# Loading two small matrices on 128 partitions, and a load split in two parts, in the opening of an attention and FFN kernel

## The chip, the cores and the metric

The kernel runs on one core of one Trainium2 chip. The metric is the time of one execution on the device in microseconds (us), lower is better; each kernel is run several times. The profile's own span is about 1.8 us shorter than that time (482.0 us for an execution of 483.81 us). In the lines below PE is the TensorE matmul engine, PEld its weight load, DVE the VectorE, ACT the ScalarE, POOL the GpSimd engine, SP the SyncE; L123 is a line of the kernel, and the line numbers shift by a few from one kernel to the next.

## The reference

```python
# batch = 8, heads = 8, seq = 1024, head_dim = 64, k_proj = 64, d_ff = 2048
k_proj = einsum('ks,bhsd->bhkd', E, k)          # E, F: 64 x 1024, float32
v_proj = einsum('ks,bhsd->bhkd', F, v)
attn   = softmax(q @ k_proj^T / 8)              # over the 64 projected keys
x      = (attn @ v_proj) as (8192 tokens, 512)
out    = relu(x @ w_in)**2 @ w_out              # 512 -> 2048 -> 512
```

## The kernel before

It works batch by batch. While the FFN of one batch runs on PE, the attention of the next one is slipped in between its products. Only the first batch has nothing to hide behind: its attention must be computed before the first FFN product. This stretch, about the first 37 us, is called the opening here. In the opening, K, V and Q of batch 0 arrive in pieces, and small "filler" products keep PE at work between them.

```python
e_f32 = []
for src in (E, F):                                    # 64 partitions, 4 KB in each
    t = relu_pool.tile([KP, S], F32, tag="h_relu", name="e_f32")
    nc.sync.dma_start(t[:], src[:])
    e_f32.append(t)
...
def load_heads(t, src, g):                            # four of the eight heads, f32 to bf16 on the way
    s = slice(4 * g, 4 * g + 4)
    nc.gpsimd.dma_start(t[:, s], rows(src, 0)[:, s])

for g in range(2):
    load_heads(K_first, k, g)
...                                                   # half of Q
for g in range(2):
    load_heads(V_first, v, g)
...                                                   # then w_in in 8 pieces, more of Q, w_out

def E_and_F():                                        # bf16, then turned so that s is on partitions
    for t, src, copy in ((ET, e_f32[0], nc.vector.tensor_copy), (FT, e_f32[1], nc.scalar.copy)):
        e_bf = soft_pool.tile([KP, S], BF16, tag="expT", name="e_bf")
        copy(e_bf[:], src[:])
        ps = ffn_psum("ps_E", (P, NI, KP), BF16)
        view = e_bf[:].rearrange("k (p i) -> k i p", i=NI)
        for i in range(NI):
            nc.tensor.transpose(ps[:, i, :], view[:, i, :], ident[0:KP, 0:KP])
        copy(t[:], ps[:])

def first_stages(self):                               # cut
    filler(2)                                         # 128 x 512 products on ET, result unused
    self.project_k(0)                                 # ps_k: 8 products on K's first half
    filler(1)
    self.transpose_k(0)
    self.project_k(1)                                 # K's second half
    filler(2)
    self.transpose_k(1)
    filler(1)
    ...                                               # Q transposes, scores, exponentials
    self.project_v(0); self.copy_v(0)                 # ps_v: 16 products on V's first half
    self.half_sums(0, apart=True); self.half_sums(1)
    self.half_reciprocals(0); self.half_reciprocals(1)
    self.half_values(0)
    self.half_normalize(0, 0, 0)                      # writes xT, which the FFN reads
    self.project_v(1); self.copy_v(1)                 # V's second half
    self.half_normalize(0, 0, 1)

def last_of_first(self):                              # called after the first three FFN products
    self.half_values(1)
    self.half_normalize(0, 1, 0); self.half_normalize(0, 1, 1)

PIECES = {                                            # batches 3 to 7: which FFN step a piece precedes
    ... 23: "sums 0, values 0 0, reciprocals 0", 26: "normalize 0 0",
    28: "scores 2, scores 3, exponentials 2", ...
}
```

The softmax here doesn't subtract the row's maximum and nothing guards it: scores larger than these inputs give would overflow.

## Time and profile before

| | before |
|---|---|
| time, median of 3 runs | 484.76 us (484.01 to 484.77) |
| PE busy | 470.4 us, 98% of the span |
| first product on K's first half | 8.61 us |
| first FFN product | 20.01 us |
| start of the 16th FFN product | 23.70 us |

The page's summary of the kernel before, first the busy time of the engines, then the chain of work that ended last:

```profile
PE 470.4 (98%) x3614; PEld 293.1 (61%) x3614; DVE 313.2 (65%) x380; ACT 261.8 (54%) x414; POOL 33.2 (7%) x46
...
PE 93%; DVE 3%; ACT 2%; DMA 1%; issue 0%; SPq 0%
```

PE is the limit, and nearly all of the waiting that is left lies in the opening. The timeline of the kernel before over its first 24 us follows. A line gives the start, the busy time (both us), engine, line, operation, what is written from what, the shape, how often, and in brackets how long the engine had been idle and what ended it.

```profile
0.74 0.58 SPq L87 DMA_DIRECT2D e_f<-in_E_dram  x1
1.25 1.64 POOL L94 DMA_DIRECT2D K_sb<-in_k_dram  x2 [0.80 <-POOLq L735]
...
4.63 0.89 DVE L137 CAST e_bf<-e_f 64x1024 bf16<-64x1024 f32 x1 [3.73 <-DMA e_f<-in_E_dram]
...
5.91 1.04 ACT L137 CAST e_bf<-e_f 64x1024 bf16<-64x1024 f32 x1 [3.89 <-DMA e_f<-in_F_dram]
...
7.64 1.03 PE L360 MATMUL ps_fill<-ET 128*128 128x512 bf16 x2
...
8.61 1.92 PE L260 MATMUL ps_k<-K_sb,ET 128*64 128x256 bf16 x8
...
11.61 1.42 PE L260 MATMUL ps_k<-K_sb,ET 128*64 128x256 bf16 x8
...
14.23 1.06 PE L295 MATMUL ps_q<-ident,Q_sb 128*128 128x128 bf16 x16
...
18.07 0.30 PE L319 MATMUL ps_att<-expT,ones 64*32 64x256 bf16 x8 [0.21 <-ACT expT L313]
...
18.58 1.06 PE L282 MATMUL ps_v<-V_sb,FT 128*64 128x256 bf16 x16
...
20.01 0.81 PE L459 MATMUL ps_h<-xT,w_in 128*128 128x512 bf16 x3 [0.37 <-DVE xT L350]
```

E and F land at about 4.6 and 5.9 us, are cast by DVE and ACT, and then turned on PE. Two fillers follow. The line for the first `ps_k` products has no bracket: PE did not wait for K, whose first half had landed at 8.25 us. Note also that eight `ps_k` products take 1.92 us in the first group and 1.42 us in the second: the clock of PE doubled within the second group (products start 213 ns apart, then, from about 12.4 us on, 109 ns). The clock row of the page does not show this; it stands at its highest digit in all 40 slices. The Trainium skill, "TensorE: Matmul & The Clock Gate", Part 1, describes this warm-up and says it needs a busy window of about 3.4 us whose phase differs from run to run; the trace agrees with the doubling.

The chain of waits of the kernel before, in order of time (start, length, what), says the same: up to 8.6 us it runs through F's load and the work on it, not through K.

```profile
1.38 4.51 DMA e_f<-in_F_dram
...
5.91 1.05 ACT e_bf L137
...
7.71 0.96 PE ps_fill L360 x2
8.68 1.86 PE ps_k L260 x8
```

### The profile page before, as it was taken

To read this page: it belongs to the slowest core of one execution; us is meant where nothing else is said; L and a number is where in the kernel's file an instruction comes from. 1 tells how busy PE (TensorE), PEld (TensorE's weight loads), DVE (VectorE), ACT (ScalarE), POOL (GpSimd) and SP (SyncE) were. 2 spreads that over 40 slices of the span, in tenths; PEclk is the share of its full clock that TensorE was granted. 3 is DMA by queue.
4 is the path that set the end of the run, shared out by engine and by line. 5 is a ranking of instruction groups with operands and counts; after the bars stand their busy time and mean duration, and the time that the engine had idled before them with its cause. 6 is when DMAs were issued, how large, how long until landed. Compare 5 with 4: busy or idle time off the path is not lost.

```text
span 482.0 us, 8383 instructions
## 1 busy us (share of the span) xinstructions
PE 470.4 (98%) x3614; PEld 293.1 (61%) x3614; DVE 313.2 (65%) x380; ACT 261.8 (54%) x414; POOL 33.2 (7%) x46
## 2 busy tenths in 40 slices
PE   4899999999999999999999999999999999999997
PEld 2544776475575746657475665747557474666656
DVE  1478855555958558493876748666594855948383
ACT  2488544758426664466635657176662756545351
POOL 6340020020020001000010000100000000000000
PEclk9999999999999999999999999999999999999999
DMA  9999989479989075931859147590712002020202
GB/s 162 204 204 207 170 184 203 124 128 227 172 124 238 6 176 89 192 80 64 145 87 229 13 121 131 90 196 1 173 3 81 20 1 88 1 88 0 88 0 88
DMA packets 72501, 55.46 MB, mean 115 GB/s; under 512 B 33936, under 2 KB 64656, under 8 KB 72464
## 3 DMA queue, kind: packets, MB, share of 16 engines
q0 software_dynamic: 30336, 29.36, 39.0%
q1 hardware_dynamic: 42128, 25.56, 21.2%
q8 instruction: 28, 0.46, 0.4%
q14 instruction: 9, 0.07, 0.0%
HBM read 59.24 MB, written 16.78 MB: 158 GB/s over the span
## 4 chain that ended last, share of the span: by engine, by line
PE 93%; DVE 3%; ACT 2%; DMA 1%; issue 0%; SPq 0%
PE ps_h L459 44%; PE ps_y L479 23%; PE ps_z L479 11%; PE ps_x L479 6%; PE ps_kv L178 3%; PE ps_att L219 2%; PE ps_att L204 2%; DVE hsq L518 1%; DMA e_f<-in_F_dram 1%; PE ps_k L260 1%; DVE s L473 1%; DVE xT L244 0%; ACT expT L313 0%; DVE xT L350 0%; ACT h_relu L510 0%; PE ps_fill L360 0%
## 5 line engine op out<-in xcount | busy, mean ns | idle before, releaser
L459 PE MATMUL ps_h<-xT,w_in 128*128 128x512 bf16 x1024 | 225.0, 379 | 0.4 <-DVE xT L350 0.4
L518 DVE TENSOR_TENSOR hsq<-h_relu 128x1024 bf16<-128x1024 f32 x123 | 150.0, 1223 | 76.7 <-ACT h_relu L510 76.1
L510 ACT ACTIVATE h_relu<-ps_h 128x512 f32<-128x512 f32 x256 | 149.8, 597 | 62.6 <-PE ps_h L459 62.4
L459 PEld LDWEIGHTS <-w_in 128*128 128x128 bf16 x1024 | 99.6, 98 | 117.9 <-issue 1.7
L479 PEld LDWEIGHTS <-s 128*128 128x128 bf16 x1024 | 98.5, 98 | 19.8 <-issue 8.7
L479 PEld LDWEIGHTS <-hsq 128*128 128x128 bf16 x768 | 73.8, 98 | 16.4 <-issue 2.9
L479 PE MATMUL ps_y<-T,s 128*128 128x256 bf16 x512 | 62.4, 273 | 0.0
L595 DVE TENSOR_TENSOR o_sb<-ps_z,p_b 128x512 f32<-128x512 f32 x16 | 11.1, 691 | 54.7 <-ACT p_b L591 21.1
L473 DVE TENSOR_TENSOR s<-hsq 128x1024 bf16<-128x1024 bf16 x64 | 43.5, 684 | 0.0
L591 ACT COPY o_sb<-ps_y 128x512 f32<-128x512 f32 x15 | 8.8, 586 | 54.2 <-PE ps_y L479 54.1
L211 ACT ACTIVATE expT<-ps_att 128x1024 bf16<-128x1024 f32 x28 | 27.2, 1025 | 14.0 <-PE ps_att L204 14.0
L244 DVE TENSOR_TENSOR xT<-ps_att,rs 128x1024 bf16<-128x1024 f32 x28 | 33.4, 1216 | 0.6 <-PE ps_att L219 0.6
L479 PE MATMUL ps_x<-w_out,hsq 128*128 128x256 bf16 x256 | 33.2, 273 | 0.0
L479 PE MATMUL ps_y<-w_out,hsq 128*128 128x256 bf16 x256 | 33.2, 273 | 0.0
L479 PE MATMUL ps_y<-T,hsq 128*128 128x256 bf16 x256 | 30.9, 272 | 0.0
L479 PE MATMUL ps_z<-T,s 128*128 128x256 bf16 x256 | 30.6, 273 | 0.0
L479 PE MATMUL ps_z<-w_out,s 128*128 128x256 bf16 x256 | 30.6, 273 | 0.0
L591 ACT COPY p_b<-ps_y 128x512 f32<-128x512 f32 (+1 forms) x17 | 9.4, 556 | 25.9 <-PE ps_y L479 25.8
L473 DVE TENSOR_TENSOR s<-s,hsq 128x1024 bf16<-128x1024 bf16 x32 | 21.9, 686 | 0.3
L473 DVE TENSOR_TENSOR s<-hsq,s 128x1024 bf16<-128x1024 bf16 x32 | 21.8, 684 | 0.0
L81 POOL DMA_DIRECT2D Q_sb<-in_q_dram x7 | 6.1, 877 | 226.1 <-DMA qT<-Q_sb 225.7
L591 ACT COPY p_a<-ps_y 128x512 f32<-128x512 f32 (+1 forms) x17 | 9.4, 561 | 21.8 <-PE ps_y L479 21.6
(74 smaller groups left out, 232.0 us busy)
## 6 DMA issues: line engine op xcount, KB each, us to landing
out_dram<-o_sb SPq DMA_DIRECT2D x30, 512.0 KB, 3.1
K_sb<-in_k_dram POOLq DMA_DIRECT2D x7, 1024.0 KB, 15.4
V_sb<-in_v_dram POOLq DMA_DIRECT2D x7, 1024.0 KB, 22.4
Q_sb<-in_q_dram POOLq DMA_DIRECT2D x7, 1024.0 KB, 9.8
w_in<-in_moe_w_in_dram POOLq DMA_DIRECT2D x8, 256.0 KB, 13.6
w_out<-in_moe_w_out_dram POOLq DMA_DIRECT2D x4, 512.0 KB, 13.3
K_sb<-in_k_dram POOLq DMA_DIRECT2D x2, 512.0 KB, 7.9
V_sb<-in_v_dram POOLq DMA_DIRECT2D x2, 512.0 KB, 12.7
```

The source lines that it names most:

```text
L178: nc.tensor.matmul(ps[0:KP, :], lhsT=ET[:, i, :], rhs=kv[:, :, i, :], start=f, stop=l)
L204: nc.tensor.matmul(ps[o, bank, :], lhsT=self.kT[r, 2 * pr + j, :], start=True, stop=True, rhs=self.qT[r, NT * (2 * pr + j):NT * (2 * pr + ...
L211: nc.scalar.activation(e[:], self.ps["s", pr][:], AF.Exp, scale=SCALE)
L219: nc.tensor.matmul(ps[32 * j:32 * j + 32, a, :], lhsT=weights(o, 4 * g + j), rhs=self.exp[2 * g + j // 2][o, bank, :], start=True, stop=Tr ...
L244: nc.vector.tensor_tensor(out=self.xT[:, 2 * g + e].rearrange("p a n t -> p a (n t)"), in0=self.ps["v", g, e][:], in1=self.rs[g][:], op=AL ...
L459: nc.tensor.matmul(ps[:], lhsT=w_in_blk(cb, fb), rhs=xT[:, cb, :, 2 * ch:2 * ch + 2], start=(cb == 0), stop=(cb == NCB - 1),)
L473: nc.vector.tensor_tensor(out=s[o][:, js], in0=x, in1=y, op=op)
L479: nc.tensor.matmul(ps[tb] if len(ps) == 2 else ps[0][:, tb], lhsT=lhs[:, j, tb * P:(tb + 1) * P], rhs=rhs[:, j], start=first and n == 0 an ...
L510: nc.scalar.activation(r[:, n], ps[:], AF.Relu)
L518: multiply = lambda: nc.vector.tensor_tensor(out=o, in0=r[:], in1=r[:], op=ALU.mult)
L591: nc.scalar.copy(to[:, t], ps)
L595: nc.vector.tensor_tensor(out=to[:, t], in0=ps, in1=more[:, t], op=ALU.add)
```

## The change

The intent: get E and F, which head that chain, in and turned sooner, by loading each on all 128 partitions (2 KB in each instead of 4 KB in 64), where the casts have half as many columns; put in two more fillers, so that PE is at work until K lands; let V's second half and the first piece of w_in arrive in two parts each, so that work can begin on the first part; and bring all four normalizing steps of the opening in front of the FFN, so that its first 16 products run in a row. Two small ones: one ReLU goes from ACT to DVE, and in the later batches "normalize 0 0" is called one FFN step earlier.

```diff
     for src in (E, F):
-        t = relu_pool.tile([KP, S], F32, tag="h_relu", name="e_f32")
-        nc.sync.dma_start(t[:], src[:])
+        t = relu_pool.tile([P, S // 2], F32, tag="h_relu", name="e_f32")
+        nc.sync.dma_start(t[:], src.rearrange("k (c s) -> (k c) s", c=2))
...
-    for g in range(2):
-        load_heads(V_first, v, g)
+    for s in (slice(0, 4), slice(4, 6), slice(6, 8)):
+        load_heads(V_first, v, s)
...
-            nc.gpsimd.dma_start(w_in_sb[j][:, g], w_in_view[:, g, :, j * fw:(j + 1) * fw])
+            for n in range(2) if (j, g) == (0, 0) else (slice(None),):
+                s = slice(n * fw // 2, (n + 1) * fw // 2) if n in (0, 1) else n
+                nc.gpsimd.dma_start(
+                    w_in_sb[j][:, g, :, s], w_in_view[:, g, :, j * fw:(j + 1) * fw][:, :, s])
...
+        pick = ident[:].rearrange("p (k c) -> p c k", c=2)
...
-            e_bf = soft_pool.tile([KP, S], BF16, tag="expT", name="e_bf")
+            e_bf = soft_pool.tile([P, S // 2], BF16, tag="expT", name="e_bf")
             copy(e_bf[:], src[:])
-            ps = ffn_psum("ps_E", (P, NI, KP), BF16)
-            view = e_bf[:].rearrange("k (p i) -> k i p", i=NI)
+            ps = ffn_psum("ps_E", (P, NI, KP))
+            view = e_bf[:].rearrange("r (p i) -> r i p", i=NI)
             for i in range(NI):
-                nc.tensor.transpose(ps[:, i, :], view[:, i, :], ident[0:KP, 0:KP])
+                for c, o in enumerate((LO, HI)):
+                    nc.tensor.matmul(ps[o, i, :], lhsT=view[:, i, :], rhs=pick[:, c, :], start=True, stop=True)
...
-            filler(2)
+            filler(4)
...
-            self.half_normalize(0, 0, 0)
-            self.project_v(1)
-            self.copy_v(1)
-            self.half_normalize(0, 0, 1)
-
-        def last_of_first(self):
+            for s in heads[1:]:                       # slice(4, 6), slice(6, 8)
+                self.project_v(s)
+                self.copy_v(s)
             self.half_values(1)
-            self.half_normalize(0, 1, 0)
-            self.half_normalize(0, 1, 1)
+            for g in range(2):
+                for e in range(2):
+                    self.half_normalize(0, g, e)
...
-        23: "sums 0, values 0 0, reciprocals 0", 26: "normalize 0 0",
+        23: "sums 0, values 0 0, reciprocals 0", 25: "normalize 0 0",
...
-                nc.scalar.activation(r[:, n], ps[:], AF.Relu)
+                if (b, ch, k, n) == (0, 0, 0, 1):
+                    nc.vector.tensor_scalar_max(r[:, n], ps[:], 0.0)
+                else:
+                    nc.scalar.activation(r[:, n], ps[:], AF.Relu)
```

## The prediction

> **What bounds it now.** TensorE. The page gives PE 98% busy; the chain of waits is 93% PE. From 37 us on, the timeline shows products back to back (0.216 us per 512 columns). Only the first 37 us and small holes later can give anything; 2% (9.7 us) is out of reach.
>
> The opening is paced by loads. DMA issues and landings, in order: K 8.25 and 10.86, Q 13.50, V 16.00 and 18.54, w_in 19.88, 21.97, 23.00, 24.29 us: 2.5 us per 512 KB, DMA share full from 4.5 us. The Trainium skill ("DMA: Bandwidth & Descriptors", Issuing engines are not separate DMA queues) says that all DMAs share the same 16 engines, so splitting a load brings no bandwidth, only an earlier first part; the trace agrees (Q's shorter rows moved at K's rate).
>
> **What the change does.**
> 1. E, F on 128 partitions: casts 0.89 (DVE) and 1.04 us (ACT) should fall to about 0.5 and 0.6; but 16 products each instead of 8 transposes, and the ET copy reads f32 (0.43 -> about 0.65). FT is ready 0.3 to 0.5 us earlier, ET about as before. Two more fillers (0.43 us each, cold) last until K lands. Steadier work may warm the TensorE clock earlier. The Trainium skill ("TensorE: Matmul & The Clock Gate", Part 1) has the clock double after a free-running busy window of about 3.4 us. The trace agrees in kind: K products start 213 ns apart until 12.2 us, 109 after. Warm at the first K group would save 0.85 us there, so the Q transposes start near Q's landing (13.55 instead of 14.23), and the first reciprocals end up to 0.7 us earlier than 19.24.
> 2. V split: but the last V part still lands at 18.5. Then products (0.45 + 0.2), copy (0.3), and DVE now does both V copies before the first normalize, which so starts at about 19.5 (before: 19.27). The first FFN product starts at about 20.2, LATER than 20.01. In exchange the second values (0.34 us at 20.75) come before it, so the 16 opening products end about 0.2 us earlier (last start 23.70 -> 23.47). The wait for the first ReLU stays; the next stage starts at about 23.9 instead of 24.11. w_in landings (24.29, 28.18) leave only 0.25 us of slack, so no more can be passed on unless the loads themselves come earlier.
> 3. w_in's first piece in halves: lands before it is needed; about 0. ReLU on DVE (about 0.7 us): first square about 0.3 us earlier, off the path.
> 4. "normalize 0 0" one step earlier in the later batches. There the second scores group waits for DVE's xT to free PSUM: the scores take 0.636 instead of 0.559 us (timeline at 166.0 us). Before the o_sb add, DVE ends it in time. 0.08 us x 5 batches = 0.39 us.
>
> **Sum.** 0.2 (opening) + 0.39 (later batches) = 0.6: 484.76 - 0.6 = 484.1 us, range 483.3 to 484.8. Chances: faster 0.01, same 0.98, slower 0.01.
>
> **Right if:** first ps_h product at about 20.2 with 16 in a row; the 37 us point about 0.2 to 0.3 us earlier; those later scores no longer wait for xT; last V landing unmoved.
>
> **Wrong if:** 2 KB rows make E and F slow and push K and all later landings back; or they speed them and all shifts up; the clock warms no earlier and fillers delay K's products; run-to-run spread (0.76 us) hides it all.

## The result, and the profile after

The changed kernel took 485.29 us (median of 5 runs, 484.52 to 485.43), the kernel before 484.76 us in the same comparison (5 runs, 484.01 to 485.00). The ratio is 1.0012, with a 95% interval of 0.9998 to 1.0025. A ratio here is always the mean time of one kernel's fast runs over that of the other's of the same rounds, so it is not quite the ratio of the medians quoted beside it. The change did not gain 0.6 us: it lost a few tenths, and the median lies outside the predicted range. The interval of this comparison just includes no change at all; that of the repetition `after_again` (below) does not.

The same stretch of the timeline, kernel after:

```profile
0.75 0.39 SPq L87 DMA_DIRECT2D e_f<-in_E_dram  x1
...
1.25 1.63 POOL L93 DMA_DIRECT2D K_sb<-in_k_dram  x2 [0.80 <-POOLq L738]
...
3.47 0.70 DVE L142 CAST e_bf<-e_f 128x512 bf16<-128x512 f32 x1 [2.56 <-DMA e_f<-in_E_dram]
...
4.18 0.62 ACT L142 CAST e_bf<-e_f 128x512 bf16<-128x512 f32 x1 [2.16 <-DMA e_f<-in_F_dram]
...
6.42 1.89 PE L364 MATMUL ps_fill<-ET 128*128 128x512 bf16 x4
...
8.92 1.87 PE L265 MATMUL ps_k<-K_sb,ET 128*64 128x256 bf16 x8 [0.61 <-DMA K_sb<-in_k_dram]
...
11.87 1.71 PE L265 MATMUL ps_k<-K_sb,ET 128*64 128x256 bf16 x8
...
14.79 1.06 PE L299 MATMUL ps_q<-ident,Q_sb 128*128 128x128 bf16 x16
...
19.08 1.08 PE L287 MATMUL ps_v<-V_sb,FT 128*64 128x128 bf16 x32
...
21.15 5.11 PE L462 MATMUL ps_h<-xT,w_in 128*128 128x512 bf16 x22 [0.19 <-DVE xT L354]
```

The first half of it is what was wanted, and more. E and F land 1.2 and 1.7 us earlier, and even with twice as many fillers PE is done with them at 8.3 us. But K's first half, issued at the same 1.25 us as before, now lands at 8.88 us, 0.63 us later than before. PE stands idle for 0.61 us and starts on K 0.31 us later than in the kernel before. The second group of K's products then takes 1.71 us instead of 1.42, because the clock doubles about 0.9 us later (by the spacing of the products between 13.15 and 13.31 us, instead of between 12.25 and 12.42). Together that is 0.56 us at the Q transposes, and it is still there when V's products begin. The chain of waits, kernel after, now starts with K's load, and after it nothing but work follows:

```profile
1.25 7.62 DMA K_sb<-in_k_dram
...
8.92 1.88 PE ps_k L265 x8
...
11.94 1.65 PE ps_k L265 x8
...
16.64 1.95 ACT expT L317 x2
...
18.63 0.52 PE ps_att L323 x24
19.15 1.03 PE ps_v L287 x32
...
20.21 0.29 DVE vp L291
20.50 0.61 DVE xT L354
...
21.15 3.61 PE ps_h L462 x16
...
30.41 23.23 DMA V_sb<-in_v_dram
```

The last line is a second place: V of batch 1 lands at 53.64 us (before 52.48), and this time PE waits for it. The two timelines at that place, before and then after:

```profile
52.44 0.40 PE L178 MATMUL ps_kv<-K_sb,ET 128*64 128x512 bf16 x1
52.53 0.38 PE L179 MATMUL ps_kv<-V_sb,FT 128*64 128x512 bf16 x1
```

```profile
53.12 0.40 PE L183 MATMUL ps_kv<-K_sb,ET 128*64 128x512 bf16 x1
53.69 0.38 PE L184 MATMUL ps_kv<-V_sb,FT 128*64 128x512 bf16 x1 [0.16 <-DMA V_sb<-in_v_dram]
```

A product on K and one on V start 0.09 us apart before and 0.57 us apart after, so this wait costs 0.48 us. One DMA engine alone makes it: fifteen of the sixteen (see "The experiments") had delivered their share of V by 52.76 us, before PE asked for it at about 53.2, and the last came 0.89 us after them. This lag is not yet there in the last load before K of batch 1 (w_out, all sixteen by 42.64 us); in between a 16 KB packet of the instruction queue began at 42.67 us and took 0.89 us. So this loss most likely belongs to that packet and not to the loads of E and F; the trace does not say which engine the packet ran on, so it is not shown. And a third place, the one that was meant to gain, does gain. In the five later batches, the scores of heads 4 to 7 no longer wait for DVE to free their PSUM (timeline of PE in batch 2, before and then after; the next product starts 0.64 us after the scores began, then 0.56 us):

```profile
165.99 0.70 PE L204 MATMUL ps_att<-qT,kT 64*64 64x512 bf16 x8
166.63 1.05 PE L479 MATMUL ps_x<-w_out,hsq 128*128 128x256 bf16 x8
```

```profile
167.14 0.63 PE L209 MATMUL ps_att<-qT,kT 64*64 64x512 bf16 x8
167.70 1.05 PE L482 MATMUL ps_x<-w_out,hsq 128*128 128x256 bf16 x8
```

How far the kernel after lags behind, when the same product of the two traces is compared: 0.69 us at 37 us, 1.15 us from 55 to 140 us, 0.76 us at 425 us, 0.72 us in the span. So the opening cost 0.69, the wait for V another 0.48, and the later scores gave 0.39 back.

### The profile page after: what moved, and what is told of

It reads as the page before. It is cut to its first block, busy times and chain, and to the rows that moved or that the text cites. A ratio compares the mean times of both kernels' runs of the same rounds, so it can differ in the third digit from the quotient of the medians.

```text
span 482.7 us, 8459 instructions
## 1 busy us (share of the span) xinstructions
PE 472.4 (98%) x3648; PEld 294.5 (61%) x3648; DVE 314.4 (65%) x382; ACT 260.9 (54%) x413; POOL 34.5 (7%) x48
## 4 chain that ended last, share of the span: by engine, by line
PE 89%; DMA 6%; DVE 3%; ACT 1%; issue 0%; POOLq 0%
PE ps_h L462 41%; PE ps_y L482 23%; PE ps_z L482 11%; PE ps_x L482 6%; DMA V_sb<-in_v_dram 5%; PE ps_kv L183 2%; PE ps_att L224 2%; PE ps_att L209 2%; DMA K_sb<-in_k_dram 2%; DVE hsq L524 1%; PE ps_k L265 1%; DVE s L476 1%; DVE xT L249 0%; ACT expT L317 0%; PE ps_kv L184 0%
## 6 DMA issues: line engine op xcount, KB each, us to landing
w_out<-in_moe_w_out_dram POOLq DMA_DIRECT2D x4, 512.0 KB, 13.2
```

## The experiments

Every load here runs on 16 DMA engines, each of which reports when its share is done; a load has landed when the sixteenth has. The Trainium skill, "DMA: Bandwidth & Descriptors", section "Why a DMA increments its semaphore by 16 and not by 1", says that these engines finish independently, and the traces show it. The sixteen completions of K's first half, sorted, read from the completion records of the traces (us):

```
before   7.51 7.53 7.58 7.65 7.65 7.70 7.71 7.73 7.77 7.78 7.91 7.92 7.95 8.04 8.22 8.25   spread 0.74
after    6.92 6.98 7.00 7.01 7.01 7.05 7.06 7.12 8.66 8.67 8.75 8.83 8.85 8.86 8.87 8.88   spread 1.96
```

After the change eight engines are done with K earlier than any was before, and eight later than any was before. K's bytes did not get slower as a whole (the mean of the sixteen is 7.81 and 7.91 us; in the four later profiles with such loads and K issued at 1.25 us it is 7.14, 7.58, 7.73 and 8.56); the engines fell out of step, and the slowest decides. Nor do they get wholly back in step: the loads queue up behind one another, and the spread of the later ones is still 1.2 to 1.3 us (V's last part 18.19 to 19.42 us; in the kernel before V's last half has 0.52). "Spread" below means the time from the first to the last of the sixteen completions of K's first half.

The theory to be tested: E and F on 128 partitions, in flight while K's load starts, put the 16 engines out of step; this delays K and everything behind it. Its rivals: the split loads and the new order of the opening cost the time (then E and F are innocent); or the spread has another cause, which the tables of each experiment name. Where an expectation calls a theory by a letter, the sentence ahead of it or the text itself says which is meant. Several expectations count on V's last landing plus some 1.7 us for the first FFN product; the section on the prediction says where that holds.

Three (`no_load`, `ef_tiny`, `ef_gap`) are single runs, and only their traces are used. Medians in us, the kernel before being run again in each batch on the same chip:

| kernel | K's 1st half lands | spread | V's last part lands | 1st / 16th FFN product | median | before, same batch | ratio (95%) |
|---|---|---|---|---|---|---|---|
| before | 8.25 | 0.74 | 18.54 | 20.01 / 23.70 | | | |
| after | 8.88 | 1.96 | 19.42 | 21.15 / 24.38 | 485.29 | 484.76 | 1.0012 (0.9998 to 1.0025) |
| ef_only | 9.53 | 2.69 | 19.87 | 21.70 / 25.39 | 485.82 | 484.06 | 1.0032 (1.0017 to 1.0048) |
| no_ef | 8.52 | 1.20 | 18.83 | 20.50 / 23.88 | 485.00 | 484.06 | 1.0014 (0.9998 to 1.0029) |
| norm_only | 8.21 | 0.82 | 18.50 | 20.34 / 24.02 | 484.27 | 484.06 | 1.0000 (0.9987 to 1.0014) |
| after_again | 9.73 | 2.98 | 20.08 | 21.78 / 25.02 | 485.19 | 484.06 | 1.0024 (1.0009 to 1.0040) |
| pool_wait | 9.64 | 2.98 | 20.15 | 21.76 / 25.44 | 486.07 | 484.86 | 1.0027 (1.0014 to 1.0039) |
| quiet | 9.88 | 3.12 | 20.15 | 24.85 / 28.54 | 488.81 | 484.86 | 1.0083 (1.0070 to 1.0096) |
| no_load | 6.90 | 0.60 | 17.37 | 18.98 / 22.67 | 482.76 | 484.86 | one run |
| norm_wait | 8.77 | 1.58 | 19.07 | 20.45 / 24.14 | 484.22 | 484.86 | 0.9994 (0.9980 to 1.0008) |
| halves | 8.45 | 1.25 | 18.73 | 20.12 / 23.82 | 484.34 | 484.25 | 0.9997 (0.9981 to 1.0012) |
| ef_late | 6.92 | 0.62 | 18.84 | 24.89 / 28.58 | 488.51 | 484.25 | 1.0078 (1.0063 to 1.0094) |
| ef_pool | 10.69 | 3.07 | 21.46 | 23.12 / 26.36 | 485.84 | 484.25 | 1.0031 (1.0013 to 1.0048) |
| f_late | 8.27 | 1.68 | 19.36 | 21.89 / 25.12 | 483.93 | 484.25 | 0.9993 (0.9977 to 1.0010) |
| rows2k | 7.94 | 0.78 | 18.24 | 20.47 / 24.15 | 484.26 | 484.33 | 0.9998 (0.9980 to 1.0017) |
| ef_tiny | 7.29 | 0.63 | 17.57 | 20.05 / 23.75 | 483.80 | 484.33 | one run |
| ef_gap | 10.52 | 0.51 | 21.31 | 23.64 / 27.34 | 487.34 | 484.33 | one run |
| halves_rest | 9.27 | 1.98 | 19.59 | 21.75 / 25.00 | 483.72 | 484.33 | 0.9986 (0.9973 to 1.0000) |
| halves_rest2 | 8.24 | 1.01 | 18.60 | 20.27 / 23.68 | 483.74 | 484.16 | 0.9994 (0.9982 to 1.0007) |
| rows2k_rest | 8.04 | 1.37 | 18.35 | 20.44 / 23.67 | 484.73 | 484.16 | 1.0009 (0.9995 to 1.0023) |

The columns on K, V and FFN products come from one profiled run each, the medians from 1 to 6 runs. A profiled run can lie at the edge of its kernel's runs: those of `halves_rest` (484.91 us), `pool_wait` and `ef_late` are their slowest, those of `after`, `no_ef`, `norm_only`, `halves`, `rows2k`, `halves_rest2` and `rows2k_rest` their fastest. The kernel before itself ranged from 483.64 to 485.60 us over the 51 runs of these five batches, with a median of 484.30.

### First question: which part of the change costs the time?

`ef_only` is the kernel before with the E and F part of the change alone, and the four fillers:

```diff
-        t = relu_pool.tile([KP, S], F32, tag="h_relu", name="e_f32")
-        nc.sync.dma_start(t[:], src[:])
+        t = relu_pool.tile([P, S // 2], F32, tag="h_relu", name="e_f32")
+        nc.sync.dma_start(t[:], src.rearrange("k (c s) -> (k c) s", c=2))
   (and the casts, the products on pick and filler(4), as in the change)
```

> The kernel before with only the E and F part of the change (128 partitions, 16 products each, four fillers). Theory D (the early end of the E and F loads makes K start into a rough stretch: K lands later although E and F land earlier): K's halves land at about 8.9 and 11.7 us, last V at about 19.4, and the time is 0.3 to 0.8 us over before. Theory S (the splitting of V and w_in is what slows the loads): K lands at 8.25 or earlier, last V at 18.5 or earlier, time equal to before or 0.1 to 0.3 us less. Theory C (chance: one DMA engine falls behind at random or by the fetch of instructions): landings unlike both, no pattern over the kernels.

It lost 1.5 us on average (ratio 1.0032), no less than the whole change (1.0012 above, 1.0024 in this batch; the intervals overlap). PE's products, kernel `ef_only`:

```profile
6.41 1.89 PE L363 MATMUL ps_fill<-ET 128*128 128x512 bf16 x4
9.57 1.87 PE L263 MATMUL ps_k<-K_sb,ET 128*64 128x256 bf16 x8 [1.27 <-DMA K_sb<-in_k_dram]
...
12.53 1.91 PE L263 MATMUL ps_k<-K_sb,ET 128*64 128x256 bf16 x8
```

PE waits 1.27 us for K, and both groups run at the slow clock, which doubles only at 15.9 us. The cause that theory C names, the fetch of instructions, drops out: apart from five packets of at most 72 bytes before 0.1 us, the traces show no packet of the instruction queues before 17.8 us in any of the twenty profiles.

`no_ef` is the kernel after with this part taken back, fillers too:

```diff
-        t = relu_pool.tile([P, S // 2], F32, tag="h_relu", name="e_f32")
-        nc.sync.dma_start(t[:], src.rearrange("k (c s) -> (k c) s", c=2))
+        t = relu_pool.tile([KP, S], F32, tag="h_relu", name="e_f32")
+        nc.sync.dma_start(t[:], src[:])
   (and the casts and transposes as in the kernel before)
-            filler(4)
+            filler(2)
```

> The changed kernel with E and F loaded and transposed as before (64 partitions, two fillers). Theory D: K at 8.25 and 10.86, last V part at about 18.5, the first FFN product at about 20.2, and the sum that I predicted for the whole change comes true: 0.5 to 0.7 us less than before. Theory S: K at about 8.9 and last V at about 19.4 us, time 0.3 to 0.7 us over before.

The profiled run shows what was expected (span 481.8 us against 482.7 after; K at 8.52 us without a wait), but it was the fastest of six, and the median of 485.00 us is a miss: no gain over the kernel before. So the six runs do not show that the rest of the change alone is a gain.

`norm_only` is the kernel before with "normalize 0 0" one step earlier in the later batches, and nothing else:

```diff
-        23: "sums 0, values 0 0, reciprocals 0", 26: "normalize 0 0",
+        23: "sums 0, values 0 0, reciprocals 0", 25: "normalize 0 0",
```

> The kernel before with only the first normalize of the later batches one step earlier. All theories: the second scores group no longer waits for xT in five batches, 0.39 us less than before (0.08 us each), landings as in before. If the time does not fall by 0.2 to 0.5 us, the gain that I read in the changed trace (delay shrinking from 1.15 us at 140 us to 0.76 us at 425 us) is not real.

The time does not resolve it (ratio 1.0000). The trace does: from the 301st to the 1024th FFN product of the first step it takes 314.89 us, the kernel before 315.28. The 0.39 us are real; the opening of this run happened to end 0.33 us later, which took most of them back (span 481.8 us, before 482.0).

`after_again` is the changed kernel a second time, to see how steady its opening is.

> The changed kernel once more, for the spread of its landings. Theory D and theory S: K again lands at 8.8 to 8.9 and 11.6 to 11.7, last V at 19.4, and V of the second batch again after it is needed. Theory C: these landings move by 0.3 us or more, and the wait of 0.35 us for V of the second batch comes or goes.

It is not steady, but late again: K at 9.73 us, spread 2.98, thirteen engines done by 8.01 us and the last three at 8.71, 9.18 and 9.73. The ratio in this batch is 1.0024. This time PE did not wait for V of batch 1, which landed at 53.36 us, because PE itself was later.

### Second question: the loads of E and F, or what is done with them?

Three runs take one suspect each out of `ef_only`. `pool_wait` is for theory P, that GpSimd's work of issuing the many later loads (the expectation calls it writing descriptors; 0.7 us and more of POOL each in the traces) disturbs K's: GpSimd waits for K's first half before it issues V and w_in.

```diff
+    hold = const_pool.tile([P, 8], BF16, name="hold")
+    nc.gpsimd.tensor_copy(hold[:], K_first[:, 0, 0:8])
```

> The E and F part alone (as ef_only), but GpSimd reads eight columns of K's first half before it issues V and w_in[...]; K's second half and Q, already issued, keep the engines busy until about 13 us. Theory P (the DMA engines fall out of step because they move K while GpSimd still writes descriptors for V and w_in): the 16 completions of K's first half lie within 0.5 us of each other, the last at about 7.3 to 7.8 us, last V at 18.0 or earlier, and the time falls by 1 us or more against ef_only (485.8). Theory Q (the early start of K itself does it): K's completions still spread over 2 us or more, last V at 19 us or later, time as ef_only.

K landed at 9.64 us all the same: fifteen engines were done by 7.52 us and one 2.1 us later. Theory P falls. `quiet` is for theory W, that the casts and products on chip disturb the loads: they wait until K's first half has landed.

```diff
+            held_e = const_pool.tile([P, 8], BF16, name="held_e")
+            copy(held_e[:], K_first[:, 0, 0:8])
             copy(e_bf[:], src[:])
```

> The E and F part alone, but the casts, and so all products and fillers on them, wait for K's first half: no work on TensorE, VectorE or ScalarE while it is loaded. Theory W (that work, 1.2 us earlier than before, disturbs the loads): K's first half lands at 8.2 us or earlier, with its 16 completions within 0.8 us. Theories P and Q: K lands at 8.9 to 9.7 us with a spread of 2 us or more, as in ef_only. In both cases the time is worse than before, as the casts start only when K is there.

K at 9.88 us, spread 3.12. Theory W falls; the lost time of this run is the wait that was put in. `no_load` doesn't load E and F at all but fills their tiles with a constant, so that its result is wrong:

```diff
-        nc.sync.dma_start(t[:], src.rearrange("k (c s) -> (k c) s", c=2))
+        nc.vector.memset(t[:], 0.03)
```

> As ef_only, but E and F are not loaded at all, their tiles are filled with a constant: a wrong result, on purpose. K's packets start with no other load beside them. Theories P and Q: K's packets start at about 3.6 us or earlier, and K's completions spread over 2 us or more, so it is not the shape of the E and F loads but that K runs early. If K's first half lands by 7.5 us with a spread under 1 us, then it is the 128-partition loads themselves that put the engines out of step (theory D).

Now K lands at 6.90 us, 5.7 us after its issue, with a spread of 0.60. All other work on E and F was still done. So it is the loads. What the profile says of K's loads from issue to landing, kernel `no_load` and then `pool_wait` (the least of the three figures is that of the first half):

```profile
DMA to landing us min/median/max: 5.7/7.5/18.6
```

```profile
DMA to landing us min/median/max: 8.4/10.1/19.7
```

`norm_wait` tried whether the kernel before gains from `pool_wait`'s hold (with the earlier normalize step); the two lines added are those of `pool_wait`.

> A candidate that may beat both: the kernel before with the earlier normalize of the later batches and with the same hold of V and w_in until K's first half has landed. Theory P: K at about 7.8 us, last V at 18.0 us, time 0.5 to 1.0 us under before. Theory Q: no change of the landings (8.2 and 18.5), time 0 to 0.4 us under before.

It does not: K at 8.77 us in the profiled run, ratio 0.9994.

### Third question: what about these loads?

`halves` is the kernel before with E on partitions 0 to 63 and F on 64 to 127 of one tile, 4 KB in each. Theory H was that a load on 64 partitions uses only half of what carries bytes into the on-chip memory, so that the two loads would not be in each other's way here.

```diff
-        t = relu_pool.tile([KP, S], F32, tag="h_relu", name="e_f32")
-        nc.sync.dma_start(t[:], src[:])
+    t = relu_pool.tile([P, S], F32, tag="h_relu", name="e_f32")
+    for n, src in enumerate((E, F)):
+        nc.sync.dma_start(t[n * KP:(n + 1) * KP], src[:])
```

> The kernel before, but F is loaded to partitions 64 to 127, beside E on 0 to 63, in rows of 4 KB as before. Theory H (E and F are slow because 64 partitions take the writes, and F at half rate for sharing E's partitions): F lands earlier than 5.9 us by 0.5 us or more, as on 128 partitions. Theory T (what spreads K is that E and F end just as K's queue starts, whatever the shape): if F lands early, K's completions spread over 2 us or more. Theory R (it is the many short rows of 2 KB): K's completions stay within 1.6 us, K's first half at 8.0 to 8.8, as in the other kernels with 4 KB rows (0.74, 1.20, 0.81, 1.58 us).

F lands only 0.26 us earlier than before, so that the two loads share partitions is not what makes them slow. Whether one load on 64 partitions is slower to write than one on 128, the other part of H, this run does not test. `ef_late` held E's and F's loads back by two memsets on DVE, to 2.52 and 3.06 us.

```diff
+        for _ in range(2):
+            nc.vector.memset(t[:], 0.0)
```

> As ef_only (128 partitions, 2 KB rows), but both loads are held back by fills of their tiles, by about 1.6 us, so that they end at about 5.0 us, as E and F of the kernel before do (4.85). Theory T (timing): K's completions lie within 1.6 us of each other and the last V lands at 18.5 to 19.0. Theory R (the shape): they spread over 2 us or more, the last V at 19.4 or later.

This went further than meant: the engines served E and F only after K's first half (they landed at 8.86 and 10.34 us), so the work on K began at 13.95 us and the run is slow. But its DMA side is telling: with K ahead of them, K landed at 6.92 us with a spread of 0.62, and all later loads stayed in step (V's last half: 0.61). `ef_pool` sent E and F through GpSimd's queue ahead of K, cast on the way, still on 128 partitions. If two queues that compete on one engine made the difference, the spread had to go.

```diff
-        t = relu_pool.tile([P, S // 2], F32, tag="h_relu", name="e_f32")
-        nc.sync.dma_start(t[:], src.rearrange("k (c s) -> (k c) s", c=2))
+        t = soft_pool.tile([P, S // 2], BF16, tag="expT", name="e_bf")
+        nc.gpsimd.dma_start(t[:], src.rearrange("k (c s) -> (k c) s", c=2))
```

> The changed kernel with E and F loaded by GpSimd ahead of K, cast to bf16 on the way: one queue carries all loads, no casts. If the spread comes from two queues that meet on the same engines, K's 16 completions lie within 0.7 us (0.6 in no_load), the last V lands at about 18.4 to 18.9 (17.4 without E and F, plus 1.3 for their bytes), and the time is about 484.3, 0.9 us less than the changed kernel. If the spread stays over 2 us, the second queue is not what does it.

It did not go: 3.07 us. A second queue is not needed. `f_late` was a try for a better kernel: E on 64 partitions ahead, F through GpSimd's queue between K and Q.

```diff
-    for src in (E, F):
-        t = relu_pool.tile([P, S // 2], F32, tag="h_relu", name="e_f32")
-        nc.sync.dma_start(t[:], src.rearrange("k (c s) -> (k c) s", c=2))
+    for src in (E,):
+        t = relu_pool.tile([KP, S], F32, tag="h_relu", name="e_f32")
+        nc.sync.dma_start(t[:], src[:])
...
+    F_bf = soft_pool.tile([KP, S], BF16, tag="expT", name="F_bf")
+    nc.gpsimd.dma_start(F_bf[:], F[:])           # issued after both halves of K
```

> A candidate: the changed kernel with E and F on 64 partitions, E alone ahead, and F, which only V's products need, by GpSimd between K and Q. Half as many bytes stand before K: K's first half at about 7.2 to 7.6, last V at 17.9 to 18.2 us, first FFN product at about 19.7, and time about 1 us under before (483.3). If E's load alone puts the engines out of step, K's spread is 2 us or more and the last V lands at 19 us or later.

No clear gain (0.9993), and a spread of 1.68 in the profiled run.

With the prediction's failed step placed in these loads but their property still open, three more runs changed one property each. `rows2k` keeps 64 partitions but cuts each row into two pieces of 2 KB, as short as those of the change:

```diff
-        t = relu_pool.tile([KP, S], F32, tag="h_relu", name="e_f32")
-        nc.sync.dma_start(t[:], src[:])
+        t = const_pool.tile([KP, 2, S // 2 + 8], F32, name=f"e_f32_{len(e_f32)}")
+        nc.sync.dma_start(t[:, :, 0:S // 2], src.rearrange("k (c s) -> k c s", c=2))
```

> The kernel before, E and F still on 64 partitions, but in rows of 2 KB (a gap of 32 bytes in the tile after each half row). If the short rows do it: K's completions spread over 2 us or more, K's first half at 8.8 us or later. If it is the 128 partitions: spread under 1.7 us and K at 8.2 to 8.8, as with 4 KB rows.

The spread is 0.78, and K and V land earlier than before (7.94 and 18.24 us): short rows alone do not put the engines out of step. They are not harmless, though: F lands at 6.75 us instead of 5.89, and PE, which has to turn it first, comes to K's products at 9.48 us instead of 8.61. Kernel `rows2k`:

```profile
6.78 1.04 ACT L137 CAST e_bf<-e_f 64x1024 bf16<-64x1024 f32 x1 [4.76 <-DMA e_f<-in_F_dram]
...
9.48 1.92 PE L260 MATMUL ps_k<-K_sb,ET 128*64 128x256 bf16 x8
```

`ef_tiny` loads only 256 bytes on each of the 128 partitions (wrong):

```diff
-        nc.sync.dma_start(t[:], src.rearrange("k (c s) -> (k c) s", c=2))
+        nc.vector.memset(t[:, 64:], 0.03)
+        nc.sync.dma_start(t[:, 0:64], src.rearrange("k (c s) -> (k c) s", c=2)[:, 0:64])
```

> As ef_only, but only an eighth of each row of E and F is loaded (256 B on each of 128 partitions; wrong result on purpose). If any load ahead of K puts the engines out of step: spread over 2 us, K at 8 us or later. If it needs the bytes in flight when K starts: spread under 1 us, K's first half at 6.9 to 7.4 us (6.9 without E and F).

The spread is 0.63: a load on 128 partitions in front is not enough, it takes its bytes. `ef_gap` loads E and F as the change does, but GpSimd issues K only when both have landed:

```diff
+    after_ef = const_pool.tile([P, 8], F32, name="after_ef")
+    for t in e_f32:
+        nc.gpsimd.tensor_copy(after_ef[:], t[:, 0:8])
```

> As ef_only, but GpSimd issues K and all that follows only after E and F have landed (at about 4.2 us). If the overlap of the loads in time does it: spread of K's completions at most 0.8 us, K's first half 5.7 us after its issue (as without E and F), that is at about 10 us. If E and F leave the engines out of step in some other way: spread over 2 us.

K is issued at 4.81 us and lands 5.7 us later, as without any load of E and F, with a spread of 0.51. Its landing times, kernel `ef_gap`:

```profile
DMA to landing us min/median/max: 5.7/7.9/19.0
```

So it takes an overlap in time. Sorted by kind, the spreads of all profiled runs are: E and F on 128 partitions and in flight with K, 1.96, 2.98, 2.69, 2.98, 3.12, 3.07; on 64 partitions and in flight with K, 0.74, 1.20, 0.82, 1.58, 1.25, 1.68, 0.78, 1.98, 1.01, 1.37; not loaded, tiny, ahead of K or behind it, 0.60, 0.63, 0.51, 0.62. The first group lies above nearly all of the second, with one run that touches it (`halves_rest` at 1.98 against `after` at 1.96), and the third group is lowest. Two limits: `rows2k`, `ef_tiny` and `ef_gap` ran on another chip than the profiles of the first group that were made for these experiments (on a chip with such profiles, `no_load` and `ef_late` say the same). And loads on 128 partitions also end earlier (4.2 us against 5.9 in the kernel before). Theory T, that their early end does it and not their shape, was to be tested by `ef_late`, which missed; no run separates the two. What inside the DMA engines hands the delay to some of them and not to others was not found.

### A version that might beat both

`halves_rest` takes the loads of E and F as in `halves`, and all the rest of the change; `halves_rest2` is the same kernel again in another batch. Against the kernel after:

```diff
-    for src in (E, F):
-        t = relu_pool.tile([P, S // 2], F32, tag="h_relu", name="e_f32")
-        nc.sync.dma_start(t[:], src.rearrange("k (c s) -> (k c) s", c=2))
-        e_f32.append(t)
+    t = relu_pool.tile([P, S], F32, tag="h_relu", name="e_f32")
+    for n, src in enumerate((E, F)):
+        nc.sync.dma_start(t[n * KP:(n + 1) * KP], src[:])
+        e_f32.append(t[n * KP:(n + 1) * KP])
   (transposes as before, filler(2))
```

> A candidate: E on partitions 0 to 63 and F on 64 to 127 in 4 KB rows, with all the rest of the change (V and w_in in parts, the new order, ReLU on VectorE, the earlier normalize). My theory (only the E and F part loses): K at 8.3 to 8.6, last V at 18.6 to 18.9, first FFN product 1.7 us later (20.3 to 20.6), 16th product 5.0 us after the last V, and 0.3 to 0.6 us less than before. Rival (the splits lose as well): equal to before or slower, by 0.3 us or more.

> The same kernel as halves_rest again. If the rest of the change is a gain of its own: 0.3 to 0.7 us under before in the fast half of its runs (483.5 to 483.8 then), ratio 0.998 to 0.9995; a profile in which K's spread is under 1.3 us has the last V at 18.6 to 18.9 us and the 16th FFN product 5.0 us later. If it was chance: ratio 1.000 or more.

Their medians are 483.72 and 483.74 us, where the kernel before had 484.33 and 484.16. In the profiled run of `halves_rest`, its slowest, the expected landings were missed (K at 9.27 us, V's last part at 19.59); those of `halves_rest2` were met. The ratios are 0.9986 and 0.9994, and both intervals reach 1: it is the best of these kernels, with a likely gain of 0.3 to 0.7 us that ten runs do not prove. PE's products, kernel `halves_rest2`:

```profile
8.28 1.90 PE L263 MATMUL ps_k<-K_sb,ET 128*64 128x256 bf16 x8
...
11.16 1.06 PE L263 MATMUL ps_k<-K_sb,ET 128*64 128x256 bf16 x8
...
20.27 6.03 PE L460 MATMUL ps_h<-xT,w_in 128*128 128x512 bf16 x25 [0.19 <-DVE xT L352]
```

K's first half is here at 8.24 us, PE doesn't wait, and the whole second group runs at the fast clock. And yet the 16th FFN product starts at 23.68 us, against 23.70 before: the part that was meant to come from V's split did not come (see the next section). The last one, `rows2k_rest`, has the loads of `rows2k` with F turned only after K's products, and the rest of the change.

```diff
-            filler(1)
+            E_or_F(1)                             # F's cast and transposes instead of a filler
...
-        E_and_F()
+        E_or_F(0)
   (loads as in rows2k)
```

> E and F on 64 partitions in 2 KB rows, F's transposes after K's instead of ahead of them, four fillers, and all the rest of the change. As in rows2k K's first half lands at about 7.9, the last V at 18.2 to 18.5; F, at 6.8 us, is no longer waited for; first FFN product at about 20.0, 16th at 23.3 (before 23.7), and with the 0.39 us of the later batches 0.6 to 0.9 us under before. If the small spread of rows2k was chance, the last V lands at 18.8 or later and the time is within 0.3 us of halves_rest2.

Its times fall in two groups, 483.29 and 483.49 against 484.73, 485.11 and 485.21 us; the profile is of the fastest one. No gain in the mean (1.0009), and why there are two groups stays open. In all, the five kernels with the rest of the change and E on 64 partitions (`no_ef`, `f_late`, `halves_rest`, `halves_rest2`, `rows2k_rest`) have ratios from 0.9986 to 1.0014, those with E and F on 128 partitions at K's side (`after`, `after_again`, `ef_pool`) from 1.0012 to 1.0031.

## Why the prediction was right or wrong, point by point

- **"Within 2%": right.** The ratio is 1.0012. (That PE is busy for 98% of the span is no strict bound: the fillers and the products at the slow clock count as busy too.)
- **Step 1, E and F on 128 partitions.** The casts came near what was costed: 0.70 and 0.62 us against "about 0.5 and 0.6". FT was ready 1.2 us earlier (its copy starts at 6.53 instead of 7.75 us), more than the 0.3 to 0.5 predicted, because the loads themselves landed earlier, which the prediction had not counted on. None of it could count, because PE then waited for K.
- **The step that failed: "unless the loads themselves come earlier", and "last V landing unmoved" as what would show it right.** The prediction moved the work on E and F but left all landings behind them where they were, so that two more fillers would "last until K lands". K's first half landed 0.63 us later, V's last part 0.88 us later. `ef_only` shows that this part alone does it (K at 9.53 us, 1.5 us lost), `no_load` and `ef_gap` that it takes the bytes of these loads, at the same time as K's. The prediction's list of risks had named the outcome, but with the wrong reason (2 KB rows that make E and F slow): here E and F got faster. On 64 partitions 2 KB rows do make F slow (`rows2k`, 6.75 us instead of 5.89), but they push neither K nor V back.
- **"Steadier work may warm the clock earlier": it warmed later.** The two added fillers end at 8.31 us, 0.57 us before K. With K at 8.25 us they would have covered the wait. The clock doubled about 0.9 us later than before and cost 0.29 us in K's second group. Over the runs, a wait for K and a late doubling go together: the seven in which PE waited for K by 0.6 us or more doubled between 13.2 and some 17 us (`after` and `f_late`), the others between 8.7 (`ef_tiny`) and 13.2 us (`norm_only`), `halves_rest2` at about 10 us; `quiet`, `ef_late` and `ef_gap`, in which the work on K was held back, are left out. The length of the wait does not order them: `after_again` waited 1.47 us and doubled at 13.6, `f_late` 0.82 us and doubled last. The page of the skill says that the window runs freely, which fits; what decided each single run was not tested.
- **Step 2, the split of V, was mis-sized as well.** Predicted: first FFN product at 20.2 us. That charged V's last landing (18.54) with 0.65 us of products, 0.3 of copy and 0.7 of normalizing. But PE only gets to V's second half when the sums and first values are done, at 18.58 us in the kernel before, and by then all of V is there (18.54). What stands in line is not the last quarter's products but all 32, 1.08 us. From the sums to the 16th FFN product it takes 5.63 us before (18.07 to 23.70) and 5.75 us after (18.63 to 24.38): the 16 in a row are there, as predicted (3.23 us from the first to the 16th start, before 3.69), but they start as much later. The split and the new order together brought 0.1 us of loss where a gain of 0.2 was predicted; no run separates the two. In runs where the clock was fast early (`no_ef`, `halves_rest2`), the same products took 1.26 and 1.33 us because PE did catch up with the load: there V's last landing is the bound, and the first FFN product came 1.67 us behind it. In the kernel after, the 32 products ran in 1.08 us without a hole, so V's late landing was not what PE waited for there; K was.
- **Step 3 (w_in's halves, ReLU on DVE): about 0, right.** The ReLU on DVE took 0.69 us as predicted, and in the kernel after no weight load of the opening waits for w_in. In the kernel before two did by 0.15 us or more, for 0.55 and 0.15 us, the first of them while PE waited for the normalize anyway.
- **Step 4, the later normalize: right, and to the digit.** 0.64 to 0.56 us in each of five batches, 0.39 us in all, shown again by `norm_only`. It is 0.08% of the time, and no comparison of times could see it; only the traces do.
- **The sum.** Predicted −0.2 − 0.4 = −0.6 us. Read from the two traces: +0.56 (K late, clock late) and +0.13 (order of the opening) at 37 us, +0.48 for V of batch 1, −0.39, together +0.78; the spans differ by 0.72. The 0.48 us was not predicted, and in `after_again` it is not there: it depends on who is later, PE or the load, and here on the one late engine named above.
- **"Run-to-run spread hides it all": partly.** The range predicted was 1.5 us wide, and the kernel before alone ranged over 2 us. The changed kernel's 11 runs lie between 484.42 and 486.38 us.

## What to carry to other kernels

A load that comes in sooner may do so at the cost of the one behind it. When all loads share the same engines and the stream is full, look at the next landing that something waits for, not at the one that was changed, and check that the sixteen completions of a load are still close together; once they have drifted apart, a good part of the lag can stay with the loads behind (in the kernel after 1.96 us, then 1.2 to 1.3; in `rows2k_rest` 1.37, then 0.59). A split load helps only where its reader would otherwise stand idle: check when the reader gets there before costing the split, and charge it with everything that then stands in line.

## What the Trainium skill lacked or had wrong

- "DMA: Bandwidth & Descriptors", section "Rules for kernel authors", advises 128 partitions for the most bandwidth, in DMAs of 1 MiB or more. For loads of 256 KB with others close behind, the runs show another side: E and F on 128 partitions landed 1.0 and 1.7 us earlier (`ef_only`), but K behind them 1.3 us later, with 1.5 us lost in the whole; on 64 partitions each (`halves`, `halves_rest`) nothing was lost (ratios 0.9997 and 0.9986).
- The same page, "Why a DMA increments its semaphore by 16 and not by 1", says that the 16 engines finish independently, but not how far apart: for K's first half 0.5 to 0.6 us where it did not meet the bytes of E and F (`no_load`, `ef_tiny`, `ef_gap`, `ef_late`), up to 3.1 us where it did (`quiet`); nor that part of a lag stays with the loads queued behind (1.2 to 1.3 us in the kernel after, from 11 to 20 us).
- The same page, "Issuing engines are not separate DMA queues", says that loads from all engines share the 16 and interleave. The traces agree (`ef_pool` has a like spread through one queue, 3.07 us, as `ef_only` through two, 2.69). No page was found that tells that such an interleaving can leave eight of the engines some 1.7 us behind the others (kernel after), or why. The runs do not tell why either, and the traces kept here do not name the engines.
- No page was found that counts instruction fetches among what delays a load: the trace shows a 16 KB packet of the instruction queue of about 0.9 us at 19.7 us (kernel before) on one engine, and w_in's second piece, of which fifteen parts landed by 21.14 us, completed at 21.97; V of batch 1 in the kernel after is a second such case (above). That the packet is the cause is inferred from time and size.
- "TensorE: Matmul & The Clock Gate", Part 1, gives the warm-up as about 3.4 us of activity with a free-running window. In these openings the doubling came anywhere from 8.7 us (`ef_tiny`, 4.1 us after PE's first product) to some 17 us (`f_late`, over 11 us after it, with waits between), so a design can't count on it to a microsecond. The clock row of the profile's page does not show the two speeds.
